# Output of two of three token tiles by Strassen's seven block products, and one set of moved K and Q, in a gated linear attention with a multiplicative FFN

## Chip, cores, metric

One core of one Trainium2 chip. The metric is the device time of one execution in microseconds; lower is better.

## The reference, cut to what matters

```python
batch, n_heads, seq, head_dim = (4, 8, 768, 48)
for t in range(S):                       # gated linear attention, complex gates a_re + i a_im
    new_re = ar * S_re - ai * S_im
    new_im = ar * S_im + ai * S_re
    kv = np.einsum('bhd,bhe->bhde', k[:, :, t], v[:, :, t])
    S_re, S_im = (new_re + kv, new_im)
    y[:, :, t] = np.einsum('bhd,bhde->bhe', q[:, :, t], S_re)
# ... x = y as (3072 tokens, 384); FFN, d_ff = 1024
a = x @ w1
b = x @ w2
h = a * b @ w3
return (h @ w_out).astype(np.float32)
```

## The kernel before

It works in eight units of 384 tokens. For each unit the gates are worked out on ScalarE and VectorE; K, Q with the gates applied are moved by DMA into tiles `KL` and `QL` with heads apart; TensorE transposes K (`tp`), forms states (`kv`), scores (`sc`) and outputs (`y`), and ScalarE copies `y` into `xT`. The FFN of a unit is eight blocks (`m`, from w1 and w2; their product goes to `ab`) and then, with w3 and w_out fused into `w3o` beforehand, one plain product for each of three tiles of 128 tokens:

```python
    def ffn_out(u, t, parts=1):
        ...
            for f in range(f0, f0 + KF // parts):          # KF = 8
                nc.tensor.matmul(out=m, lhsT=ab_t[u][:, f, t * P:(t + 1) * P], rhs=w3o[:, f],
                                 start=(f == 0), stop=(f == KF - 1))
            if f == KF - 1:
                o = two.tile([P, DM], FP, tag="o", name="ot")
                nc.scalar.copy(out=o, in_=m)
                ...                                        # store
```

The order on TensorE is written by hand. While a unit's attention runs, the FFN of the unit before is cut into its pieces: the first `AHEAD[u]` pieces come first, the rest is spread over the pieces of the attention (`tr`: transposes, `kv`, `sc`, `y`). A step of the next unit's gates is queued after each. Other engines' queues are ordered by a scheduler ahead of time, and each engine works through its queue in that order.

```python
    AHEAD = [0, 0] + [3] * (NU - 2)
    # for odd units:
        return [[tr[0][0]], [tr[0][1]], [tr[1][0], kv[0]], [tr[1][1]], [kv[1]], sc[0], sc[1] + [y[0]],
                sc[2] + [y[1]], [y[2]]]
    def unit(u, steps, rest, look, ahead):
        for f in rest[:ahead]:
            f()
            next(steps, None)                              # a step of the next unit's gates
        rest = rest[ahead:]
        ...
            for f in rest[first[i]:first[i + 1]] + p[i]:
                f()
                next(steps, None)
            next(look, None)                               # a piece of the weight check
```

`look` loads the raw float64 weights once more, up to 0.5 MB at a time, and checks them on ScalarE, in two or three instructions a piece (its first six pieces check the gates of the first two units in the same way); the kernel takes a general path if a check fails. Odd units had a second set of `KL` and `QL`:

```python
        KL = head_pool[u % 2].tile([2 * D, H, TT + 1], FP, tag="KL", name="KL")
        QL = head_pool[u % 2].tile([2 * D, H, TT], FP, tag="QL", name="QL")
```

## Time and profile before

| | before |
|---|---|
| device time, median (range) of 4 runs | 590.55 us (589.48 to 592.74) |
| profiled run: device time, span | 587.98 us, 586.2 us |
| TensorE busy, ScalarE busy, VectorE busy | 552.6, 351.0, 306.6 us |

The prediction below shows the lines of the page, the stretches and the timelines. Beside them, the waits of TensorE (what it waited for: us in total, times, longest; the line of 20.0 us that belongs to loading the weights is left out, here and in the lists below):

```profile
PE tp L652 <- DVE gR L616: 3.2, 1, 3.2
PE m L722 <- ACT xT L693: 1.5, 1, 1.5
PE sc L664 <- DVE A L666: 1.5, 4, 0.6
```

After the 120 us of loading there is little to be won by removing waits: one of 3.2 us, and some small ones. The rest is TensorE's own work.

### The profile page before, as it was taken

The numbers are of one execution on the slowest core, as the hardware profiler recorded it, in microseconds if no ns is written. First come the engines' busy times: TensorE is split into PE (matmuls) and PEld (weight loads), VectorE is DVE, ScalarE is ACT, GpSimd is POOL, SyncE is SP. The second block draws the span as 40 slices with busy tenths as digits, with TensorE's granted clock in tenths as the row PEclk, the third lists the DMA queues.
The fourth block names the chain that finished last, engine by engine and source line by source line (L and its number), as shares of the span: only waits on it lengthen the run. The fifth ranks groups of instructions, "written<-read, shape, count | busy, mean of one in ns | idle before, by whom it ended". The sixth has DMA issues, their size and how long they took to land.

```text
span 586.2 us, 8856 instructions
## 1 busy us (share of the span) xinstructions
PE 552.6 (94%) x3514; PEld 365.7 (62%) x3514; DVE 306.6 (52%) x426; ACT 351.0 (60%) x576; POOL 3.5 (1%) x9
## 2 busy tenths in 40 slices
PE   4569899999979999999999999999999999999996
PEld 2235675568546765677567756776667756765553
DVE  5899488845851676159413585257514683310110
ACT  5898658456673799378834888599836553101100
POOL 2000000000000000000000000000000000000000
PEclk9789999999999999999999999999999999999999
DMA  7877998385165349934852538853851017000001
GB/s 221 285 284 278 236 325 277 108 172 140 55 160 137 85 129 287 232 112 122 222 155 83 161 102 206 234 175 117 216 140 28 15 35 154 1 15 29 0 1 45
DMA packets 46338, 84.71 MB, mean 145 GB/s; under 512 B 4688, under 2 KB 36176, under 8 KB 45392
## 3 DMA queue, kind: packets, MB, share of 16 engines
q1 hardware_dynamic: 46288, 84.06, 50.7%
q8 instruction: 29, 0.48, 0.3%
q14 instruction: 21, 0.17, 0.1%
HBM read 60.42 MB, written 4.72 MB: 111 GB/s over the span
## 4 chain that ended last, share of the span: by engine, by line
PE 72%; DMA 9%; DVE 8%; ACT 6%; issue 2%; SPq 2%; ACTq 0%; DVEq 0%
PE m L722 34%; PE o L738 19%; PE y L691 5%; DMA raw<-in_w_dram 5%; PE sc L664 5%; PE kv L702 4%; DMA vr<-in_v_dram 3%; PE f L859 2%; PE tp L652 2%; ACT re L544 1%; SPq L485 1%; DMA re<-in_a_re_dram 1%; DVE gZ L600 1%; ACT low L764 1%; ACT low L766 1%
## 5 line engine op out<-in xcount | busy, mean ns | idle before, releaser
L722 PE MATMUL m<-xT,w1s 128*128 128x384 f32 x384 | 134.9, 488 | 1.5 <-ACT xT L693 1.5
L722 PE MATMUL m<-xT,w2s 128*128 128x384 f32 x384 | 134.4, 486 | 0.0
L738 PE MATMUL o<-w3o,ab 128*128 128x384 f32 x384 | 129.9, 491 | 0.0
L728 DVE TENSOR_TENSOR ab<-m,a 128x384 f32<-128x384 f32 x64 | 35.6, 557 | 135.7 <-PE m L722 117.7
L722 PEld LDWEIGHTS m<-xT,w2s 128*128 128x128 f32 x384 | 72.9, 190 | 51.1 <-ACT a L727 0.5
L738 PEld LDWEIGHTS o<-w3o,ab 128*128 128x128 f32 x384 | 71.2, 190 | 49.0 <-issue 4.0
L722 PEld LDWEIGHTS m<-xT,w1s 128*128 128x128 f32 x384 | 70.5, 190 | 44.6 <-ACT xT L693 2.1
L727 ACT COPY a<-m 128x384 f32<-128x384 f32 x64 | 30.5, 478 | 69.9 <-PE m L722 69.7
L859 PE MATMUL f<-wo_s,w3s 128*128 128x384 f32 x128 | 49.3, 544 | 20.0 <-DVE wo_s L775 20.0
L654 ACT COPY KT<-tp 128x384 f32<-128x384 f32 x40 | 33.5, 848 | 41.1 <-PE tp L652 41.1
L859 PEld LDWEIGHTS f<-wo_s,w3s 128*128 128x128 f32 x128 | 26.6, 214 | 40.0 <-DVE wo_s L775 21.8
L664 PE MATMUL sc<-QL,KL 96*128 96x128 f32 x384 | 47.7, 277 | 2.3 <-DVE A L666 1.5
L664 PEld LDWEIGHTS sc<-QL,KL 96*128 96x128 f32 x384 | 45.6, 192 | 6.2 <-DVE A L666 2.3
L666 DVE COPY_PREDICATED A<-causal,sc 128x512 f32<-128x512 int32 x48 | 34.3, 736 | 18.2 <-PE sc L664 17.9
L691 PE MATMUL y<-A,V 128*32 128x128 f32 x768 | 39.3, 275 | 0.1
L691 PEld LDWEIGHTS y<-A,V 128*32 128x32 f32 x768 | 32.9, 109 | 5.5 <-issue 2.0
L691 PE MATMUL y<-QL,T 96*32 96x128 f32 x640 | 34.6, 272 | 0.0
L702 PEld LDWEIGHTS kv<-V,KT 128*96 128x96 f32 x320 | 29.6, 165 | 3.2 <-ACT KT L654 1.2
L691 PEld LDWEIGHTS y<-QL,T 96*32 96x32 f32 x640 | 31.3, 110 | 0.0
L702 PE MATMUL kv<-V,KT 128*96 128x64 f32 x320 | 30.0, 246 | 0.9 <-ACT KT L654 0.9
L742 ACT COPY ot<-o 128x384 f32<-128x384 f32 x24 | 11.3, 470 | 32.4 <-PE o L738 32.4
L544 ACT ACTIVATE re<-gZ 128x1152 int32<-128x1152 f32 (+3 forms) x20 | 19.2, 969 | 18.3 <-DVE gZ L600 14.6
(98 smaller groups left out, 586.2 us busy)
## 6 DMA issues: line engine op xcount, KB each, us to landing
look<-in_w_dram SPq DMA_DIRECT2D x28, 512.0 KB, 4.4
raw<-in_w_dram SPq DMA_DIRECT2D x7, 1024.0 KB, 7.9
raw<-in_w_dram SPq DMA_DIRECT2D x8, 768.0 KB, 7.3
KL<-gR SPq DMA_DIRECT2D x24, 192.5 KB, 3.2
KL<-k SPq DMA_DIRECT2D x24, 192.5 KB, 3.6
re<-in_a_re_dram SPq DMA_DIRECT2D x24, 192.0 KB, 6.0
im<-in_a_im_dram SPq DMA_DIRECT2D x24, 192.0 KB, 3.9
k<-in_k_dram SPq DMA_DIRECT2D x24, 192.0 KB, 4.5
```

The source lines that it names most:

```text
L544: chain(nc.scalar.activation(**kw))
L652: nc.tensor.transpose(out=tp[:, f], in_=src[:, f, c * C:(c + 1) * C], identity=ident)
L654: nc.scalar.copy(out=KT_t[u, c][:, :, :, x].rearrange("p h d f -> p f d h"), in_=tp.rearrange("p f (d h) -> p f d h", h=H))
L664: nc.tensor.matmul(out=sc[:, j], lhsT=KL[:, x * n + j, w], rhs=QL[:, x * n + j, w], start=True, stop=True)
L666: nc.vector.copy_predicated(out=A[:, x * n:(x + 1) * n], data=sc, mask=causal.rearrange("p (h t) -> p h t", h=1).to_broadcast([P, n, C]))
L691: nc.tensor.matmul(out=o, lhsT=a, rhs=b, start=s0, stop=s1)
L702: nc.tensor.matmul(out=kv[:, hd], lhsT=KT[:, hd].rearrange("p d x f -> p (d x f)"), rhs=V[:, hd], start=True, stop=True)
L722: nc.tensor.matmul(out=m, lhsT=w[:, j * P // WB, f, j * P % WB:j * P % WB + P], rhs=xT_t[u][:, f], start=(f == 0), stop=(f == KD - 1))
L727: copied[:] = [nc.scalar.copy(out=a, in_=got[0])]
L728: nc.vector.tensor_tensor(out=ab_t[u][:, j], in0=got[1], in1=a, op=OP.mult)
L738: nc.tensor.matmul(out=m, lhsT=ab_t[u][:, f, t * P:(t + 1) * P], rhs=w3o[:, f], start=(f == 0), stop=(f == KF - 1))
L859: nc.tensor.matmul(out=sums[j], lhsT=w3_t[f][:, j * P:(j + 1) * P], rhs=w3_t["wo"][:, f], start=(f == 0), stop=(f == KF - 1))
```

## The change

Intent: less TensorE work. Two of a unit's three token tiles (units 1 to 7) are taken as a 2 x 2 block product (tokens 2 x 128, inner 2 x 512, columns 2 x 192) and formed with seven block products instead of eight, at the price of sums on VectorE. The room for the sums comes from giving up the second set of `KL` and `QL`. The order constant goes from three blocks ahead to four.

```diff
-    AHEAD = [0, 0] + [3] * (NU - 2)
+    AHEAD = [0, 0] + [4] * (NU - 2)
...
-        KL = head_pool[u % 2].tile([2 * D, H, TT + 1], FP, tag="KL", name="KL")
-        QL = head_pool[u % 2].tile([2 * D, H, TT], FP, tag="QL", name="QL")
+        KL = one.tile([2 * D, H, TT + 1], FP, tag="KL", name="KL")
+        QL = one.tile([2 * D, H, TT], FP, tag="QL", name="QL")
...
+    def out_weights():                       # once: four differences of blocks of w3o
+        ...
+            nc.vector.tensor_tensor(out=T[:, i], in0=x, in1=y, op=OP.subtract)
+    def out_sums(u):                         # four sums of blocks of ab
+        ...
+                nc.vector.tensor_tensor(out=S[:, i], in0=x, in1=y, op=op)
+    def out_pair(u):
+        def product(n, i, p):
+            if i == 0:
+                m["bank"] = ps_m.tile([P, 2, DH], FP, tag="mm", name="p")
+            m[p] = m["bank"][:, i]           # two products share a PSUM bank
+            for f in range(KH):              # KH = 4
+                nc.tensor.matmul(out=m[p], lhsT=a[:, f], rhs=b[:, f], start=(f == 0), stop=(f == KH - 1))
+            ...                              # two copies on ScalarE, nine adds on VectorE, two stores
+        return [lambda n=n, p=p: product(n, n % 2, p) for n, p in enumerate((1, 6, 7, 5, 2, 4, 3))]
...
-        return [... ffn_ab ...] + [p for t in range(UC) for p in ffn_out(u, t, parts)]
+        last = ffn_out(u, UC - 1)[0]
+        return [... ffn_ab ...] + [lambda: (out_sums(u), last())] + out_pair(u)
```

Cut: the operand lists, and the gate loads, which are now issued just ahead of the K and Q loads.

More of the change, by code (lines that the diff above doesn't have):

```diff
@@ L450 @@
     ps_m = fast.enter_context(tc.tile_pool(name="ps_m", bufs=4, space=PSUM))
-    gate_pool, head_pool = [one, None], [one, None]
+    gate_pool = [one, None]
     Ab = [singles.tile([P, H, C], FP, name=f"A{i}") for i in range(2)]
@@ L641, in gates @@
         if 1 < u + 1 < NU:
+            load_gates(u + 1)
             load_qkv(u + 1)
@@ L728, in ffn_ab @@
             nc.vector.tensor_tensor(out=ab_t[u][:, j], in0=got[1], in1=a, op=OP.mult)
+    KH, DH = KF // 2, DM // 2
+    s_t = {}
+    def out_weights():
+        T = s_t["T"] = late.tile([P, 4, KH, DH], FP, tag="T", name="To")
+        B = [[w3o[:, i * KH:(i + 1) * KH, j * DH:(j + 1) * DH] for j in range(2)] for i in range(2)]
+        for i, x, y in ((0, B[0][1], B[0][0]), (1, B[1][1], T[:, 0]), (2, B[1][1], B[0][1]), (3, B[1][0], T[:, 1])):
+            nc.vector.tensor_tensor(out=T[:, i], in0=x, in1=y, op=OP.subtract)
+        s_t["B"] = B[0][0], B[1][0], B[1][1], T[:, 3], T[:, 0], T[:, 1], T[:, 2]
@@ new lines, in out_sums @@
+    def out_sums(u):
+        S = s_t["S"] = late.tile([P, 4, KH, P], FP, tag="S", name="So")
+        A = [[ab_t[u][:, i * KH:(i + 1) * KH, t * P:(t + 1) * P] for i in range(2)] for t in range(2)]
+        with tc.high_priority():
+            for i, x, y, op in ((0, A[1][0], A[1][1], OP.add), (1, S[:, 0], A[0][0], OP.subtract),
+                                (2, A[0][0], A[1][0], OP.subtract), (3, A[0][1], S[:, 1], OP.subtract)):
+                nc.vector.tensor_tensor(out=S[:, i], in0=x, in1=y, op=op)
+        s_t["A"] = A[0][0], A[0][1], S[:, 3], A[1][1], S[:, 0], S[:, 1], S[:, 2]
@@ new lines, in out_pair, with add, done @@
+    def out_pair(u):
+        m, U, o = {}, {}, {}
+        def add(out, x, y):
+            nc.vector.tensor_tensor(out=out, in0=x, in1=y, op=OP.add)
+        def done(t):
+            r0 = u * TT + t * P
+            nc.sync.dma_start(out=out[r0:r0 + P, :], in_=o[t])
+        def product(n, i, p):
+            if i == 0:
+                m["bank"] = ps_m.tile([P, 2, DH], FP, tag="mm", name="p")
+            m[p] = m["bank"][:, i]
+            a, b = s_t["A"][p - 1], s_t["B"][p - 1]
+            for f in range(KH):
+                nc.tensor.matmul(out=m[p], lhsT=a[:, f], rhs=b[:, f], start=(f == 0), stop=(f == KH - 1))
+            if n == 0:
+                for t in range(2):
+                    o[t] = two.tile([P, DM], FP, tag="o", name="ot")
+                for x in (2, 3, 4):
+                    U[x] = late.tile([P, DH], FP, tag=f"U{x}", name="U")
+            with tc.high_priority():
+                if p == 6:
+                    nc.scalar.copy(out=U[2], in_=m[1])
+                    add(U[2], m[6], U[2])
+                elif p == 7:
+                    add(U[3], m[7], U[2])
+                elif p == 5:
+                    add(U[4], m[5], U[2])
+                    add(o[1][:, DH:], m[5], U[3])
+                elif p == 2:
+                    nc.scalar.copy(out=o[0][:, 0:DH], in_=m[1])
+                    add(o[0][:, 0:DH], m[2], o[0][:, 0:DH])
+                elif p == 4:
+                    add(o[1][:, 0:DH], m[4], U[3])
+                    done(1)
+                elif p == 3:
+                    add(o[0][:, DH:], m[3], U[4])
+                    done(0)
+        return [lambda n=n, p=p: product(n, n % 2, p) for n, p in enumerate((1, 6, 7, 5, 2, 4, 3))]
@@ L904, in ffn @@
     def ffn(u, parts=1):
-        return [lambda j=j: ffn_ab(u, j) for j in range(KF)] + [p for t in range(UC) for p in ffn_out(u, t, parts)]
+        if u == 0:
+            return [lambda j=j: ffn_ab(u, j) for j in range(KF)] + [p for t in range(UC) for p in ffn_out(u, t, parts)]
+        last = ffn_out(u, UC - 1)[0]
+        return [lambda j=j: ffn_ab(u, j) for j in range(KF)] + [lambda: (out_sums(u), last())] + out_pair(u)
     def unit(u, steps, rest, look, ahead):
@@ L973 @@
                 phase.close()
-                head_pool[1] = fast.enter_context(tc.tile_pool(name="late_heads", bufs=1))
             if i < 6:
@@ L979 @@
                     pass
-                load_gates(2)
-        late = fast.enter_context(tc.tile_pool(name="late", bufs=2))
-        look = check_weights(late)
+        late = fast.enter_context(tc.tile_pool(name="late", bufs=1))
+        look = check_weights(fast.enter_context(tc.tile_pool(name="looks", bufs=2)))
+        out_weights()
         for u in range(1, NU):
@@ L987 @@
                 pass
-            if u + 2 < NU:
-                load_gates(u + 2)
         for _ in look:
```

## The prediction

> **What bounds the kernel now.** I read the page first (busy time, the 40 slices, the chain), then the stretches unit by unit, then the timelines of single units. A unit is one of eight half-sequences of 384 tokens; its attention on TensorE is woven into the feed-forward block (FFN) of the unit before it.
>
> ```profile
> span 586.2 us, 8856 instructions
> PE 552.6 (94%) x3514; PEld 365.7 (62%) x3514; DVE 306.6 (52%) x426; ACT 351.0 (60%) x576; POOL 3.5 (1%) x9
> ...
> PE   4569899999979999999999999999999999999996
> ...
> PE 72%; DMA 9%; DVE 8%; ACT 6%; issue 2%; SPq 2%; ACTq 0%; DVEq 0%
> PE m L722 34%; PE o L738 19%; PE y L691 5%; DMA raw<-in_w_dram 5%; PE sc L664 5%; PE kv L702 4%; DMA vr<-in_v_dram 3%; PE f L859 2%; PE tp L652 2%; ACT re L544 1%; SPq L485 1%; DMA re<-in_a_re_dram 1%; DVE gZ L600 1%; ACT low L764 1%; ACT low L766 1%
> ```
>
> After the weights are in (about 120 us) TensorE has work without a break, and the output product L738, which the change shortens, is 19% of the chain. The stretches of single units say how tight that is (columns: PE, PEld, DVE, ACT, POOL busy):
>
> ```profile
> 155.00:219.50 64.50, 60.98 (x411) 41.20 (x410) 36.80 (x42) 44.32 (x79) 0.00 (x0) 1.00 0.49 127
> 219.50:281.70 62.20, 62.20 (x430) 41.78 (x429) 34.31 (x41) 45.96 (x74) 0.00 (x0) 1.00 0.69 195
> 281.70:345.60 63.90, 63.60 (x420) 42.93 (x419) 28.09 (x33) 42.56 (x75) 0.00 (x0) 1.00 0.49 135
> 345.60:407.00 61.40, 61.40 (x426) 41.09 (x425) 33.25 (x39) 50.93 (x95) 0.00 (x0) 1.00 0.64 179
> ```
>
> Units 3 and 5 have no TensorE idle at all, unit 4 has 0.3 us, unit 2 has 3.5. So TensorE time saved is worth its face value there, as long as nothing else becomes late. What could become late stands in the timelines of two places in units 4 and 5:
>
> ```profile
> 318.21 1.16 ACT L544 ACTIVATE gA<-re 128x1152 f32<-128x1152 f32 x1
> ...
> 343.38 0.48 ACT L693 COPY xT<-y 128x384 f32<-128x384 f32 x1
> ...
> 355.14 1.36 DVE L616 TENSOR_TENSOR gR<-k,re 128x1152 f32<-128x1152 f32 x1 [3.18 <-ACT re L544]
> ...
> 357.18 0.49 PE L652 MATMUL tp<-ident,gR 128*128 128x128 f32 x3
> ```
>
> The gates of the next unit start on ScalarE at 318.2, as this unit's scores begin; the copy xT, which the next unit's FFN needs, comes out behind them in the queue at 343.9, 3.7 us after its product y ended (340.2); and gR is ready at 356.5, 0.7 us before TensorE transposes it. These two margins are covered today by long TensorE work, and the change shortens that work.
>
> **What the skill says.** (1) "TensorE: Matmul & The Clock Gate", "Wait — 56ns, not 53.3ns?": start to start is N/2.4 GHz plus about 2.5 ns when warm. The trace agrees if a float32 matmul counts as two records, each taking two cycles a column: starts are 323 ns apart at 384 columns (768/2.4 = 320), 109 at 128 (transposes). (2) Same page, "Step-by-step: what each phase is for": the queue pulls weight loads ahead of running matmuls. Agrees: score products load new 128-column weights for every 128-column pass and still start 112 ns apart. (3) "PSUM — Partial Sum Buffer", "PSUM bank collisions raise a hardware error": two engines may not touch one bank at once, so accesses must be ordered. The trace of before cannot show it (each bank there holds one product), but the built program of after makes the second product in a bank wait for VectorE's read of the first. (4) "VectorE: DVE Perf Modes", "Mode 2×_2P": a float32 tensor_tensor runs at one element a cycle. Agrees: 1152 elements start 1267 ns apart, 1200 at 0.96 GHz plus 67.
>
> **The change part by part.**
> Removed: for units 1 to 7, two token tiles, each of 8 matmuls x 2 records x 323 ns = 5.17 us; 10.34 us a unit.
> Added: seven products of 4 matmuls x 2 records at 192 columns. Interpolated between 109 (128) and 323 (384), a record takes 109 + 214 x 64/256 = 162.5 ns, and the weight load (112 at most) stays hidden: 56 x 162.5 = 9.10 us. Gain 1.24 us a unit, 8.7 us for seven. The bubbles of about 0.1 us on entering and leaving the 32-column products y stay as many as they are.
> VectorE gains four sums of 512 columns (533 + 67 = 0.60 us each) and nine adds of 192 columns (a 384-column one from PSUM takes 0.56, so about 0.36): 2.4 + 3.2 = 5.6 us a unit, in about 62, where it is busy 22 to 37. ScalarE trades two copies of 384 (0.47) for two of 192 (about 0.28): -0.4 us. The four differences of the output weights (768 columns, 0.87 us each, once) are queued among the gates of unit 1; most of it fits in gaps where VectorE waits for ScalarE: +0.5 us.
> The operand sums lie hidden: the last tile's plain product (5.17 us) and the first product (1.3) stand between the last ab and the first use of a sum, and the sums need about 2.8 us.
> One set of K and Q: the moves of the next unit now wait for this unit's last scores and outputs. In the trace the moves of unit 4 are issued at 283.4, after the last y of unit 3 had ended at 276.4, and are read at 318.6. Cost zero.
> The start of transposes: with four FFN blocks ahead instead of three, and twelve pieces spread over the unit instead of eight, transposes come after five blocks (19.4 us), not three (11.6). In unit 2 TensorE waited 3.2 us for gR (the waits: PE tp <- DVE gR 3.2, once); 7.7 us more work ahead covers it: -3.2 us.
> Between the first and second score groups there now is a product of 1.3 us. In even units there was nothing, and TensorE waited 0.46 us there for VectorE's copy (gap 575 ns in place of 112); four times: -1.8 us.
> The last unit's products run back to back, so the fourth and sixth wait for VectorE to empty their bank: the record's tail (163 ns), 0.36 of add and about 0.1 of signalling, 0.6 us each, +1.2 us. This eats that unit's gain.
> Sum without new stalls: 591.1 - 8.7 - 3.2 - 1.8 + 0.5 + 1.2 = 579.1 us.
>
> **New stalls, worked out from the queues' order.** From the start of the gates to the end of the last y TensorE now has: three score groups 5.6, three y 5.8, products 7, 5, 2: 3.9; 15.3 us, and then only products 4 and 3 (2.6) before the next unit's first FFN product. Before it was 21 to 25 and then 5.2. I added up ScalarE's queue in the built order, from the first gate instruction to the third xT, by the starts' distances in the trace (gate 1.1 to 1.15, checks 1.24, weight checks 0.57 to 0.75, copies 0.36): 15.8, 16.2, 15.8, 17.6, 15.2 us for units 2 to 6. The same sum for before gives 22.2, 26.8, 21.1, 24.8 where the trace has 27.3, 33.0, 25.6, 27.6, so waiting adds 3 to 6. With 3, because the stretch is shorter, xT comes at 18.2 to 20.6 against 17.9: stalls of about 1, 1, 1, 2.7 and 0.3, 6 us together. In even units the predicated copy before the last y sits behind a gate operation, and the adds of products 4 and 3 sit behind the scans: perhaps 0.5 us each time, partly the same wait.
> Second margin: from the gates' start to the transposes there were 38 (even) to 43 us (odd), now 15.3 + 2.6 + 19.4 = 37.3. ScalarE's sum to its last needed sine is 31.0, 32.2, 32.5, 36.6, 24.5; with the 3 to 6 of waiting and 1.4 for VectorE gR is ready at 35.4 to 41. Only unit 5 to 6 is clearly over, by 3, most of which the xT stall of the same boundary has given already. I add 0.5 in all. I take X = 6 us of new stalls: 585 us.
>
> **Rivals.** (a) No new stalls: the scheduler has already ordered the queues for the shorter stretch, xT is never late: 579 us. For it: the piece sums lie close to 17.9. Against: in before, ScalarE's queue ran 3 to 6 us over its sum. (b) ScalarE's queue becomes the bound: gates, weight checks and copies of 46 to 51 us in a unit of 60, bunched after the scores, so each of five boundaries loses 2.5 to 3.5 us at xT or at the transposes: 591 to 594, the gain is gone. For it: the 0.7 us of margin at 357. Against: later transposes. (c) Weight loads bound the 192-column passes: their records last 190 ns, longer than 162.5; were that a rate, the products would take 10.6 us and the gain would turn into 0.3 us of loss a unit: about 595. Against it: the same 190 ns records start 112 apart in the scores. (d) Each second product waits 0.6 us for its bank in every unit: two more waits x 6 = 7 us, 592. Against: in the units the scores and y stand between, except before product 4, where y (1.9 us) is longer than the add.
>
> **Range and chances.** All of (a) gives 579, (b) alone 592; a mixture of small stalls is likeliest. Prediction 585, range 578 to 592. Over 2% faster means below 579.3, which needs no stall at all: 0.12. Slower than 603 needs (b) and (c) together: 0.02. Within 2%: 0.86.
>
> **What would show each step.** Records of the products 162 to 163 ns apart, not 190: the gain of 1.24. The wait of tp for gR in unit 2 gone, and no wait of scores for K. In the waits of PE: m for ACT xT growing from 1.5 us to about 6; the fourth and sixth product waiting for VectorE only in the last unit, 1.2 us together; tp for gR below 2 us. Units of 60 to 62.5 us in place of 61.4 to 64. If the waits of m and tp together exceed 10 us, (b) is right and I am wrong; if they stay under 2 us, I am too high by about 5.

## The result

| | before | after |
|---|---|---|
| device time, median (range) of 4 runs | 590.55 us (589.48 to 592.74) | 583.02 us (581.98 to 583.88) |
| ratio (95% interval) | | 0.9867 (0.9833 to 0.9902) |
| profiled run: device time, span | 587.98, 586.2 us | 583.44, 581.6 us |

A ratio here is the mean time of one kernel's fast runs over that of the other's of the same rounds, so not quite the ratio of the medians. The change is 1.3% faster: within 2%, but clear of noise.

Lines of the page of after (first and second part, and the chain):

```profile
span 581.6 us, 9282 instructions
PE 546.8 (94%) x3682; PEld 388.0 (67%) x3682; DVE 341.3 (59%) x507; ACT 348.5 (60%) x576; POOL 3.5 (1%) x9
...
PE 64%; ACT 13%; DMA 11%; DVE 8%; issue 3%; SPq 0%; ACTq 0%; DVEq 0%
```

TensorE is 5.8 us less busy and still at 94%; in the chain that ended last, ScalarE rose from 6% to 13%. The reader should take this as a hint that ScalarE now holds TensorE up in places. The waits of TensorE after:

```profile
PE m L723 <- ACT xT L694: 3.1, 3, 1.8
PE m L723 <- ACT a L728: 2.4, 2, 1.8
PE tp L653 <- DVE gR L616: 1.6, 1, 1.6
PE sc L665 <- DMA QL<-q: 1.4, 1, 1.4
...
PE p L768 <- DVE ot L756: 0.5, 1, 0.5
...
PE p L768 <- DVE U L756: 0.5, 1, 0.5
```

The stretches of units 2 to 5 (columns: PE, PEld, DVE, ACT, POOL busy, granted clock, DMA share, GB/s):

```profile
153.10:216.20 63.10, 62.51 (x443) 45.76 (x442) 34.55 (x46) 40.34 (x73) 0.00 (x0) 1.00 0.45 115
216.20:277.80 61.60, 61.13 (x455) 44.74 (x453) 35.66 (x49) 42.47 (x71) 0.00 (x0) 1.00 0.66 180
277.80:342.10 64.30, 62.48 (x443) 46.08 (x444) 37.58 (x51) 46.86 (x82) 0.00 (x0) 1.00 0.58 158
342.10:404.10 62.00, 61.13 (x454) 44.74 (x453) 34.23 (x47) 45.01 (x81) 0.00 (x0) 1.00 0.59 165
```

Unit 2 has become 4.2 us shorter, unit 3 0.6; unit 4 has become 0.5 longer though its TensorE work is less: it has 1.8 us of idle that it did not have. The lengths of all units, from the first FFN record of one unit to that of the next, as read from each trace (the last column runs to the end of the span; the kernels not named yet are experiments below):

| us | u1 | u2 | u3 | u4 | u5 | u6 | u7 | last FFN |
|---|---|---|---|---|---|---|---|---|
| before | 63.5 | 67.3 | 62.2 | 63.8 | 62.3 | 63.8 | 62.4 | 52.2 |
| before, profiled again | 63.4 | 69.0 | 62.2 | 63.8 | 62.3 | 63.8 | 62.4 | 52.2 |
| order of after, plain products | 63.3 | 64.3 | 63.2 | 63.4 | 63.3 | 63.4 | 62.4 | 52.2 |
| after | 64.0 | 63.1 | 61.6 | 64.3 | 62.0 | 64.0 | 61.2 | 52.4 |
| after, profiled again | 64.0 | 63.1 | 61.2 | 62.2 | 61.7 | 64.0 | 61.2 | 52.7 |
| after, no weight checks | 64.0 | 63.1 | 60.9 | 62.1 | 60.9 | 62.1 | 61.2 | 52.4 |

The products themselves behave as the prediction said: in the trace their records start 162 or 163 ns apart (median 163; the interpolation gave 162.5). In the last FFN, where nothing stands between them (TensorE's timeline: start, length, line, what, count, and in brackets the idle time before and who ended it), this reads:

```profile
566.73 2.76 PE L768 MATMUL p<-To,So 128*128 128x192 f32 x16
569.94 1.57 PE L768 MATMUL p<-To,So 128*128 128x192 f32 x8 [0.45 <-DVE U L756]
571.35 1.46 PE L768 MATMUL p<-w3o,ab 128*128 128x192 f32 x8
573.32 1.57 PE L768 MATMUL p<-To,ab 128*128 128x192 f32 x8 [0.51 <-DVE ot L756]
```

Products 6 and 7 run through; the fourth and the sixth wait for VectorE to read the other half of their bank. From start to start these gaps are 0.61 and 0.67 us longer than a record, and the first record after each of them takes 0.10 us more (266 and 267 ns in place of 162).

The longest new wait is in unit 4. First ScalarE's timeline, then TensorE's:

```profile
300.50 0.69 ACT L877 ACTIVATE look<-look 128x512 f32<-128x512 f32 x1 [3.42 <-DMA look<-in_w_dram]
301.21 1.28 ACT L548 ACT_TABLE_LOAD   x1
302.51 0.74 ACT L878 ACTIVATE look<-look,consts 128x512 f32<-128x512 f32 x1
...
303.25 0.46 ACT L728 COPY a<-m 128x384 f32<-128x384 f32 x1
```

```profile
303.76 2.20 PE L723 MATMUL m<-xT,w1s 128*128 128x384 f32 x6 [1.82 <-ACT a L728]
```

ScalarE stood 3.4 us at a weight check whose load had not landed. The copy that frees a PSUM bank for TensorE was behind it in the queue, and behind a table load (for the next unit's gates) and a second check, 2.75 us in all from the end of the wait to the copy; its product had ended at about 299.7, so it came some 3.6 us late, and TensorE waited. No new arithmetic is in this chain. In the second profile of after that check waited 0.44 us in place of 3.42, and unit 4 has no such stall: its length is 62.2 us.

### The profile page after: what moved, and what is told of

The parts are those of the page before. It is cut to its first block, busy times and chain, and to the rows that moved or that the text cites. A ratio compares the mean times of both kernels' runs of the same rounds, so it can differ in the third digit from the quotient of the medians.

```text
span 581.6 us, 9282 instructions
## 1 busy us (share of the span) xinstructions
PE 546.8 (94%) x3682; PEld 388.0 (67%) x3682; DVE 341.3 (59%) x507; ACT 348.5 (60%) x576; POOL 3.5 (1%) x9
## 4 chain that ended last, share of the span: by engine, by line
PE 64%; ACT 13%; DMA 11%; DVE 8%; issue 3%; SPq 0%; ACTq 0%; DVEq 0%
PE m L723 34%; PE p L768 9%; PE o L803 7%; DMA raw<-in_w_dram 5%; PE kv L703 4%; PE sc L665 4%; PE y L692 3%; DMA look<-in_w_dram 3%; PE tp L653 2%; DMA vr<-in_v_dram 2%; ACT gZ L544 2%; ACT gR L544 2%; ACT re L544 1%; DVE gA L576 1%; DVE gZ L600 1%
## 5 line engine op out<-in xcount | busy, mean ns | idle before, releaser
L924 PE MATMUL f<-wo_s,w3s 128*128 128x384 f32 x128 | 51.0, 559 | 18.4 <-DVE wo_s L840 18.4
L803 PE MATMUL o<-w3o,ab 128*128 128x384 f32 x160 | 53.8, 487 | 0.0
L803 PEld LDWEIGHTS o<-w3o,ab 128*128 128x128 f32 x160 | 29.6, 190 | 18.9 <-issue 0.4
L710 DVE TENSOR_TENSOR T<-kv,T 96x512 f32<-96x512 f32 x16 | 11.0, 687 | 42.4 <-PE kv L703 42.4
L768 PE MATMUL p<-To,So 128*128 128x192 f32 x168 | 31.5, 331 | 0.5 <-DVE U L756 0.5
```

The costliest lines, as they stand in the source:

```text
L768: nc.tensor.matmul(out=m[p], lhsT=a[:, f], rhs=b[:, f], start=(f == 0), stop=(f == KH - 1))
L924: nc.tensor.matmul(out=sums[j], lhsT=w3_t[f][:, j * P:(j + 1) * P], rhs=w3_t["wo"][:, f], start=(f == 0), stop=(f == KF - 1))
```

## Experiments

### 1. The order alone

```diff
 kernel before
-    AHEAD = [0, 0] + [3] * (NU - 2)
+    AHEAD = [0, 0] + [4] * (NU - 2)
```

> The kernel before with only the order constant changed: four FFN blocks ahead of a unit's attention instead of three. If the shorter time comes from the Strassen products alone, this is within 1 us of before. By my theory the wait of the transposes for gR in unit 2 (3.2 us) goes, the rest stays (the three gaps of 0.46 us between score groups too): 3 to 3.5 us faster, ratio about 0.994.

Measured: 590.06 us (588.09 to 594.62), ratio to before 1.0032 (0.9989 to 1.0074). My expectation was wrong. The waits of TensorE of this kernel:

```profile
PE kv L702 <- ACT KT L654: 2.6, 4, 0.9
PE m L722 <- ACT a L727: 1.7, 2, 1.1
PE m L722 <- ACT xT L693: 1.3, 1, 1.3
...
PE tp L652 <- DVE gR L616: 0.2, 1, 0.2
```

The wait for gR did go (3.2 to 0.2), but with the same eight large pieces and one more of them ahead, transposes and state products have nothing between them, and TensorE waits for the copies that lie between instead. Unit 2 does become 2.3 us shorter than before (65.0), but units 3 and 6 become 1.5 and 1.3 longer. The order constant alone gives nothing; together with the finer pieces it does (experiment 6).

### 2. One set of moved K and Q alone

```diff
 kernel before, with the one-set hunks of the change and its earlier gate loads
```

> The kernel before with one set of moved K and Q and the gate loads moved, but neither products nor order changed. By my theory it costs nothing: ratio 0.999 to 1.001, no wait of scores or moves added. If sharing the set had a cost that the change merely paid for elsewhere, this would be slower by 1 us or more.

Measured: 591.47 us (589.57 to 592.62), ratio 1.0019 (1.0000 to 1.0039), just outside what I expected. In its profile units 3, 5, 6 and 7 are as long as before to 0.2 us; unit 4 has 0.7 us more (0.3 of it a wait for the copy `a`), unit 2 the slower clock of experiment 8. A cost of up to 0.4% is not excluded, but no wait for the moves of K and Q was added (the scores of unit 1 waited 0.7 us, against 0.8 before).

### 3 and 4. Weight checks left out, after and before

```diff
-            unit(u, ..., look if u > 1 else iter(()), AHEAD[u])
+            unit(u, ..., iter(()), AHEAD[u])
-        for _ in look:
-            pass
         judge()
```

The result is still right on these inputs, but the kernel is no longer a valid one: it would not notice weights that it cannot convert. With the weight checks go the gate checks of the first two units; in all 164 records of ScalarE and 19 MB of loads.

> The changed kernel without the weight checks (on these inputs the result is the same): some 36 x 2 to 3 instructions less in ScalarE's queue and 16 MB less to load. Theory: the new stalls of TensorE in units 3 to 6 (for xT 0.6 and 1.0, for a copy 1.8, for gR 1.7 us) come from ScalarE's queue being full of checks, so they go, all or nearly all: 4.5 to 5.5 us faster than the changed kernel, about 578. Rival: the gates' own dependency chain sets these stalls, then under 1.5 us is gained.

> The kernel before without the weight checks. Theory: TensorE is the only bound there after 120 us, so taking the same ScalarE work away gains under 1 us (ratio 0.998 to 1.0). If ScalarE's queue already cost time before, it gains as much as in the changed kernel.

Measured on one chip: after without checks 578.7 us (577.73 to 580.17), ratio to before 0.9821 (0.9800 to 0.9843); before without checks 590.52 us, ratio 1.0017 (0.9988 to 1.0046). In spans the first is 576.0 us, 5.6 below the first profile of after and 4.0 below the second. The timed runs show less than I expected: 0.9821 against 0.9867 and 0.9846 (experiment 9) for after, some 1.5 to 2.7 us, from different rounds and with intervals that overlap. So what follows rests on the profile. Its units 2 to 6:

```profile
153.30:216.40 63.10, 62.49 (x444) 45.76 (x443) 35.06 (x47) 32.49 (x47) 0.00 (x0) 1.00 0.37 92
216.40:277.30 60.90, 60.90 (x453) 44.80 (x452) 37.32 (x50) 30.17 (x42) 0.00 (x0) 1.00 0.38 98
277.30:339.40 62.10, 62.10 (x444) 45.93 (x443) 36.08 (x49) 33.06 (x46) 0.00 (x0) 1.00 0.39 97
339.40:400.40 61.00, 61.00 (x455) 44.91 (x454) 37.41 (x50) 30.23 (x42) 0.00 (x0) 1.00 0.39 98
400.40:462.50 62.10, 62.10 (x444) 45.94 (x443) 36.10 (x49) 31.88 (x44) 0.00 (x0) 1.00 0.28 68
```

Units 3 to 6 have no TensorE idle left, and their lengths are 1.2, 1.7, 1.4 and 1.7 us under those of before: the 1.24 us of the products, and in even units the 0.46 us of the gap between scores. So both gains are real and whole, and what took part of them away in after is the work of the checks on ScalarE or their loads. The same removal did nothing for the kernel before. The rival, that the gates' own chain alone sets the stalls, falls by the profile: the chain is still there, and the stalls are not. Not separated is that without the checks the scheduler may also order the other queues differently.

### 5. The change with three blocks ahead

```diff
 kernel after
-    AHEAD = [0, 0] + [4] * (NU - 2)
+    AHEAD = [0, 0] + [3] * (NU - 2)
```

> The changed kernel with three FFN blocks ahead as before, so transposes start after four blocks instead of five. In the changed kernel gR is ready 1.6, 1.0, 1.4, -1.7 (waited) and 0.8 us before the transposes of units 3 to 7; with 3.9 us less, TensorE waits about 2.3, 2.9, 2.5, 3.9 and 3.1 us more at transposes, up to 14 us, unless a stall elsewhere moves: 588 to 597, no gain left over before. If the order constant does not matter, within 1 us of the changed kernel.

Measured: 599.65 us (596.94 to 599.70), ratio 1.0148 (1.0109 to 1.0187): slower than before, and just over my range. The waits:

```profile
PE tp L653 <- DVE gR L616: 13.8, 4, 5.4
```

The total is the 14 us foreseen, but in four waits, not five: unit 4 has none, unit 5 has 5.4. Over that, four to eight matmul records after three of the four waits start 640 ns apart instead of 323; with the records at their edges this costs some 6 us together; see experiment 8. In this order the gates have a shorter stretch in which to finish, and the longer lead pays for it; without the lead the change is a loss. How much of this is due to the products and how much to the finer pieces is not shown: plain products in parts with three blocks ahead were not run.

### 6. The order and storage of the change with plain products

```diff
 kernel after
-        return [... ffn_ab ...] + [lambda: (out_sums(u), last())] + out_pair(u)
+        return [... ffn_ab ...] + [last] + [p for t in range(2) for p in ffn_out(u, t, 4)]
```

> The changed kernel with its order, its single set of K and Q, but the two tiles computed plainly again, in eight pieces of two matmuls (1.29 us each, as long as a product). TensorE has 8.7 us more work, 1.2 us less of waiting in the last unit; part of the ScalarE stalls (6 us) is covered by the longer work. Theory: 4 to 7.5 us slower than the changed kernel, 587 to 590.5. If Strassen's sums and adds cost as much as its products save, it is equal to the changed kernel.

Measured: 586.51 us (585.46 to 588.04), ratio to before 0.9948 (0.9912 to 0.9985). So order and finer pieces give about 0.5% and the products about 0.8% more (0.9867/0.9948 = 0.9919; the two ratios come from different rounds). By the table of units, what the order gives is in unit 2 (67.3 or 69.0 to 64.3); what the products give is in units 2, 3, 5 and 7, about 1.2 to 1.6 us each. In units 1, 4, 6 and the last FFN the products lose, 0.2 to 0.9 us, to stalls and, in unit 1, to the differences of the output weights: in this kernel, which does not form them, the scores of unit 1 wait 0.7 us, in after 1.4, for the moves of `QL`.

### 7. Banks of their own in the last unit

```diff
 kernel after
+            if u == NU - 1:
+                pool, tag = ((ps_s, "sc"), (ps_v, "v"), (ps_m, "mm"))[min(n // 2, 2)]
+                m[p] = pool.tile([P, DH], FP, tag=tag, name="p")
```

> The changed kernel with a bank of its own for each of the seven products of the last unit. Theory: the two waits of TensorE for VectorE's read of the first product of a bank (0.61 and 0.67 us at 570 and 573 us) go: 1.2 to 1.3 us faster, ratio 0.998. If they come from something else, no change.

Measured: 580.40 us (579.46 to 583.42), ratio to before 0.9854 (0.9814 to 0.9895). The interval does not tell it from after, but the profile does: both waits for VectorE are gone from TensorE's waits and the last FFN takes 51.2 us in place of 52.4, the 1.2 us foreseen.

### 8. The kernel before again

No edit.

> The kernel before once more, unchanged, to see how far two runs of one kernel lie apart and whether the profiled run of before (587.98 us, under its timed runs of 589.5 to 592.7) was a quick one: ratio 1.000 within 0.3%, profile 586 to 591 us, differences in the first 120 us, where weights and gates are loaded.

Measured: 589.76 us (588.54 to 590.04), ratio 0.9992 (0.9958 to 1.0025). The profile was 1.6 us longer, but my guess of where was wrong: not in the loading, but in unit 2. The stretch around the wait for gR, first in the first profile of before, then in this one:

```profile
160.00:175.00 15.00, 11.78 (x42) 6.90 (x41) 9.02 (x11) 11.56 (x19) 0.00 (x0) 1.00 0.61 153
```

```profile
160.00:175.00 15.00, 11.75 (x36) 6.72 (x35) 8.96 (x11) 11.34 (x18) 0.00 (x0) 0.89 0.62 153
```

And TensorE's timeline of the second:

```profile
167.07 0.60 PE L652 MATMUL tp<-ident,gR 128*128 128x128 f32 x3 [3.25 <-DVE gR L616]
167.46 3.75 PE L722 MATMUL m<-xT,w1s 128*128 128x384 f32 x6
171.05 2.10 PE L722 MATMUL m<-xT,w2s 128*128 128x384 f32 x6
```

After the wait the granted clock (the column after POOL) was lower in the mean, 0.89, and six records took 3.75 us instead of 2.10. Of four profiles with the order of before that have this wait of some 3.2 us (before, this one, experiments 2 and 4), three show the slow records, and their unit 2 is 1.7 to 2.9 us longer. So the 3.2 us wait cost 4.9 to 6.1 us in these three, and the first profile of before had been the lucky one. This is the likely reason why the times differ by 7.5 us and the two profiles by 4.6; it is not shown, because the timed runs left no traces.

### 9 to 12. Attempts at a faster valid version

```diff
 e9: kernel after, unchanged
 e10: kernel after
-            next(look, None)
+            if i % 2 == 0 or u == NU - 1:      # every second piece; the rest in unit 7 and the last FFN
+                next(look, None)
 e8: e10, and the banks of experiment 7, and out_weights() called after unit 1
 e11: kernel after, with the banks of experiment 7
-            next(look, None)
+            for _ in range(2 if i < 2 else int(i < 5)):
+                next(look, None)
-    nc.sync.dma_start(out=raw[...], ...)
+    nc.gpsimd.dma_start(out=raw[...], ...)
```

> The changed kernel once more, as the yardstick for the two runs beside it: ratio to before 0.985 to 0.989. In its profile the stalls of TensorE for xT, for a copy and for gR in units 3 to 6 add to 3 to 6 us, at other places than in the first profile where a wait on a load of the weight checks happened to be long.

> The changed kernel with the weight checks thinned out: every second piece in units 2 to 6, the rest in unit 7 and in the last FFN, where ScalarE is nearly idle. Theory: as the stalls come from checks in ScalarE's queue, about half to three quarters of the 4 to 5 us that leaving them out gave are won, so 2 to 3.5 us faster than the changed kernel: 579.5 to 581. If only the load from HBM mattered and not the queue, nothing is won.

> The same thinned checks, with banks of their own in the last unit (1.2 us) and the differences of the output weights formed after unit 1 instead of among its gates (0.6 us: TensorE waited 1.6 us for the moves of unit 1 in place of 0.9): 577 to 579.5, ratio to before 0.978 to 0.982, with all outputs checked as in the kernel before.

Measured on one chip: after again 580.85 us (580.00 to 581.81), ratio to before 0.9846 (0.9818 to 0.9873), just below what I expected; checks spread 582.27 us, 0.9865 (0.9835 to 0.9895); spread with the rest 582.63 us, 0.9865 (0.9835 to 0.9895). Nothing was won. Spreading moved the stalls: in the last of these, TensorE waits 5.7 us for xT (three times) where after again has 2.2, the longest as unit 7 ends, where there are no gates and where I had put checks. There ScalarE waits for a load once more. The differences of the output weights were still made at the same place in VectorE's queue: the scheduler filled a gap with them, whatever the program's order, so that edit tested nothing.

> The changed kernel with the same weight checks moved: their loads go out on GpSimd's queue instead of standing behind the moves and the K loads on SyncE's, and they are made in the first half of each unit, between the fifth FFN block and the scores, where ScalarE is half idle and no gate work is queued; the last unit's products have banks of their own. Theory: with no check between a gate instruction and the copy of xT, and none waiting for a late load, the stalls for xT, copies and gR go as they did when the checks were left out (576.0 us in that profile), and 1.2 us more in the last unit: 575 to 578, ratio to before 0.975 to 0.981. If the queue of ScalarE is not what makes the stalls, or the loads on the other queue come no earlier, it stays at 580 to 583, as the thinned checks did.

Measured: 603.48 us (602.14 to 606.27), ratio 1.0219 (1.0190 to 1.0248), a clear miss. The waits for gR are gone, and the ones for xT fell to one of 1.8 us. But with two load buffers and checks back to back, ScalarE itself waits for the loads. ScalarE's waits, then TensorE's:

```profile
ACT look L881 <- DMA look<-in_w_dram: 42.3, 17, 6.5
...
ACT look L881 <- DMA look<-in_w_out_dram: 13.4, 4, 5.5
```

```profile
PE tp L653 <- ACT KT L655: 9.9, 6, 2.9
PE kv L703 <- ACT KT L655: 9.4, 6, 3.1
```

TensorE now waits for the copies of the transposes, 19.3 us, which stand behind those checks. The edit changed two things at once, the place of the checks and the queue that issues their loads; which of them made the loads late is not separated. Together with e10 this says what the checks do: a check whose load is late holds every copy behind it, wherever it is put. Leaving the checks out took away both their waiting for loads and their own run time. The traces separate the two in part. The 1.8 us of unit 4 had a late load before it, and it is gone in the second profile, where that load was only 0.4 us late. The wait of 1.6 us for gR in unit 6 stands in three profiles (after, after again, experiment 7); there, in the first, no check waited for a load from 396 us to the wait's end at 425, while checks ran for some 8.5 us from 404 on, so this one is put down to the checks' run time. The share of the rest stays open. No version here is shown to be faster than after; the banks of experiment 7 shorten the last FFN and are the only edit worth keeping.

## Why the prediction was right, point by point

- **The gain of the products, 1.24 us a unit:** right. Records 162 to 163 ns apart; without stalls units 3 and 5 are 1.2 and 1.4 us shorter. Rival (c), weight loads as a bound, falls: those records lasted 190 ns here too.
- **Sums on VectorE hidden:** right; no wait of TensorE for a sum appears. A sum's record lasted 0.69 us, and in the last unit sums start 0.73 us apart, not 0.60, where each needs the one before; an add lasted 0.35 to 0.36.
- **One set of K and Q, cost zero:** not clearly contradicted (experiment 2: 1.0019, from 1.0000 to 1.0039).
- **Differences of the output weights, +0.5 us:** right. They start 0.85 to 1.00 us apart (0.87 foreseen), and unit 1 came out 0.5 us longer than before, 0.7 longer than in experiment 6, which forms none.
- **The wait in unit 2, -3.2 us:** the wait went, but it was mis-sized. I had not seen the lower clock after it, which cost 1.7 to 2.9 us in three of four profiles of that order. And the order constant alone does not bring it (experiment 1).
- **Gaps between scores, -1.8 us:** a little high. The gaps of 0.46 us are gone, but the trace of before has only three of them (units 2, 4 and 6), not the four counted: 1.4 us.
- **The last unit, +1.2 us:** a little low: 0.61 + 0.67, and 0.1 us more on the record after each wait, 1.5 in all. Experiment 7 took 1.2 to 1.3 of it away, so the shared bank was the cause. (That each bank of before holds one product, as the prediction says, is loose: a bank of scores holds several, read after the last of them.)
- **New stalls, 6 us:** the total was right (5.3 us of idle in the first profile), the parts were not. At xT I had put nearly all; it was 0.5 us in unit 3 and 0.9 in unit 5, so that the waits for xT came to 3.1 us and not to 6. Transposes waited 1.6 us for gR, in the unit I had named, where I had added 0.5. And 2.4 us were waits that I had not thought of, for the copy `a` that frees a PSUM bank: 1.8 us in unit 4, behind a check that waited for its load, and 0.6 in unit 2, behind a gate instruction that waited for VectorE. The step that failed was to add run times along ScalarE's queue and to take each wait on it as short. Against the kernel without checks, units 3 to 6 are 5.7 us longer in the first profile of after and 2.9 in the second, so the total was in part luck. The units came out at 61.2 to 64.3 us, not at 60 to 62.5.
- **Sums:** rival (b) is added up wrongly: five boundaries at 2.5 to 3.5 us give 591.6 to 596.6, not 591 to 594, and in the second margin unit 5 to 6 is over by 3.7 us on its own numbers, not by 3. Neither changes the prediction.

The sum was 585 us; the medians of after are 583.0 and 580.9. Part of the 2 to 4 us between is where the sum started: at 591.1, while the rounds with these runs have 590.6 and 589.2 for before, so 6.1 us were forecast and 7.5 and 8.3 came. The rest may be the lower clock in unit 2, which only kernels with that wait had, and stalls smaller in some runs; the timed runs left no traces that could show it.

## What to carry to other kernels

When TensorE is the bound and busy all the time, less of its work is worth its face value, but its long stretches were also the cover under which other engines' queues caught up: count what each queue has to do in the shortened stretch, and lengthen the lead where it is short. In a queue worked in order, an instruction that waits for a load is as long as that load is late, and everything behind it pays. A wait of TensorE of 2.3 to 3.3 us can cost 1.6 to 2.9 us more at the lower clock after it (experiments 5 and 8 and the spread checks), and at times costs nothing more.

## What the Trainium skill lacked or had wrong

- "TensorE: Matmul & The Clock Gate", "What's actually happening", gives the half clock after at least one idle window of about 3.4 us. Here waits shorter than that were followed by passes at half speed: one of 2.45 us (experiment 5), one of 2.33 (the spread checks of e8: three records 640 ns apart, one at 801 before them and one at 594 after), and those of about 3.25 us in three of four profiles. The same page calls the window free-running, which fits that it does not come every time; but 3.4 us of idle is not a safe lower limit.
- The same page, "Wait — 56ns, not 53.3ns?", gives start-to-start times that fit one cycle a column, and no page gives measured ones for float32. In these traces a float32 matmul is two records, and their starts fit two cycles a column: 109 ns at 128, 162.5 at 192, 323 at 384 columns.
- No page gives the time of going over to products of 32 stationary columns and back. Here the next record starts 93 ns later on entering (205 in place of 112 after scores, 416 in place of 323 after `o`). On leaving, the first full-width record follows the last of them after 200 ns, and the second follows the first after 427 ns in place of 323. That last 0.1 us also stands on the first record after a wait (266 in place of 162 in the last FFN).
